# The opening of a Fourier-mixing and ELU kernel: batch 0 folded by mirrored rows first, and its order of work written anew

## The chip, the cores and the metric

The kernel runs on one core of a Trainium2 chip. The metric is device time in microseconds (us) of one execution. The engines are TensorE (PE, matmuls), VectorE (DVE), ScalarE (ACT), GpSimd (POOL) and SyncE (SP, which here issues most of the DMA transfers). Each engine takes its instructions from a queue of its own in the order in which the program wrote them; waits between engines go by semaphores.

## The reference

```python
X = np.fft.fft(x, axis=1)              # x: 8 batches, 3008 rows, 256 channels
X = np.fft.fft(X, axis=2)
y = X.real.reshape(24064, 256)
h = y @ w_in                           # 256 x 2048
g = np.where(h > 0, h, np.exp(np.minimum(h, 0)) - 1)
out = g @ w_out                        # 2048 x 256
```

Two facts are used. The real part of the two-dimensional transform depends only on x[s, d] + x[-s, -d], rows and channels taken modulo 3008 and 256. And it is even under (k, c) -> (-k, -c), so half of the output rows can be had from the other half by a sum and a difference. The weights come as 64-bit floats and are converted in the kernel.

## The kernel before

**Transform along the rows.** A batch is loaded as four tiles L[0] to L[3] (`xl0` to `xl3`), each 128 partitions by six rows of 256 channels: row s ahead from 0, rows back from 3008, rows back from 1504, rows ahead from 1504. L[0] and L[3] are loaded by SP; L[1] and L[2], whose rows run backwards, by GpSimd's indirect DMA (line 239). Each tile comes in two transfers, one of four rows of a partition (512 KB) and one of two ("few", 256 KB). The tiles are *folded* over channels (e: channel d plus channel 256-d, o: the difference) and over the four quarters of the rows, giving four tiles of 128 by 768: cosine and sine, for even and odd output rows. Each is then multiplied with its matrix `MC` (four matrices, 128 by 1887 columns) in two halves of three products: "even" (189, 189 and 378 columns) and "odd" (three of 377 or 376 columns). Channel 128 has a transform of its own, `x`, with one column as the stationary operand. The results are unfolded by VectorE (copy, sum, up, down) into rings `Rr`, `Ir` and `Rb` of eight tiles of 256 columns.

**Transform along the channels** is folded into the weights: every chunk of 256 columns of w_in (eight chunks, w0 to w7) is multiplied with a small matrix `CC` (step f), and the result is copied by ScalarE into `Ws` and `Wc`; its last row goes to `wex`.

**Weights.** A chunk is loaded as pairs of 32-bit words and converted by a chain: top (a) and mantissa (b) on VectorE, power (p), low (l) and high (d) on ScalarE, round (R), sign (s) and multiply (M), pair (P). Round and multiply are on GpSimd for all chunks but w0, whose chain is on VectorE and ScalarE. The chunks of w_out are u0 to u7. `w0a` is the top of chunk w0, `f0` its product with CC, `Wc0` and `Ws0` the copies, `wm0` and `wex0` its last row. Buffers for raw words and powers are shared among chunks, so that a chunk can wait for one before it.

**Steps.** The rest is 376 steps (tile of 256 tokens times slice of 256 hidden columns, eight slices per tile): P (Wc times Rr), V (the even part E on VectorE, `even_part`, line 1263), Q (Ws times Ir, added to P), h (2E minus the sum), b+ and b- (ReLU of the negative, ScalarE), x+ and x- (exponential, ScalarE), g+ and g- (ELU, VectorE), and then Xa and Xb, the products with w_out. For the first two tiles these are plain; from the third on a Winograd form with sums on GpSimd. In the first sixteen steps the two first tiles alternate.

**Order.** Every operation is a function put into a list with a due time in us; the list is sorted by due time and written out, each function pinned in program order. `PERIOD` (4.8) is the length of a step. For the opening, the table `FRONT` gives 40 due times from -20.84 to 33.32 with the names of operations; what stands ahead of it, written directly, are 46 warm-up matmuls on zeros, the loads of batch 0, w0, CC and the first matrix, and w1. The other loads (`load_rest`) stand at -11.63 behind a one-element copy on ScalarE that reads the last of the loaded rows. Later chunks of weights get their steps at offsets -0.5, 0.05, 0.06 and 2.95 from a step's start. Batch 1 is folded on GpSimd (`mirror_folds`), by mirrored rows first; batches 2 to 7 by a finer split of the rows.

The folds of batch 0 in `fold_x` go over channels first, each tile for itself (e0 to e3, o0 to o3, 768 columns each, e0 and e2 cut in two), then over rows (E0, E2, O0, O2 between two tiles, EO0 to EO3 between the pairs), all on VectorE. `mm` is the helper of all matmuls (line 539), `vtt` (545), `gtt` (548) and `act` (551) those of VectorE, GpSimd and ScalarE.

Of the kernel before, what the change touches and what calls it, by code (L numbers as in the profile page):

```python
# [9 lines left out]
FP = mybir.dt.float32  # L10
# [5 lines left out]
ALU = mybir.AluOpType  # L16

SEQ = 3008
ND = 256
# [15 lines left out]
BS = 4  # L35

# [126 lines left out]
def kernel(  # L163
# [64 lines left out]
    def load_x(b):  # L228
# [20 lines left out]
        def ahead(j, row):  # L249
            nc.sync.dma_start(out=L[j][:, 0 : 4 * ND], in_=xrows(b, row, 4, 128, 4))  # L250
            nc.sync.dma_start(
                out=L[j][:, 4 * ND :], in_=xrows(b, row + 512, 2, 128, 2)
            )

        loads = [lambda n=n: back(2 - n // 2, n % 2) for n in range(4)]
        return L, loads + [lambda: ahead(3, HALF), lambda: ahead(0, 0)]
# [238 lines left out]
    def load_mats(ri, kodd, cuts=()):  # L495
        n = (2 * ri + kodd) * BW
        ends = (0, *cuts, BW)
        for a, z in zip(ends, ends[1:]):
            nc.sync.dma_start(
                out=MC[ri, kodd][:, a:z], in_=MC_dr.ap()[:, n + a : n + z]  # L500
            )
# [128 lines left out]
    def fold_x(L, engine_of, cuts_of):  # L630

        ops = {}

        def op(key, o, a, b, f):
            tt = lambda o, a, b, f: pin(
                engine_of(key).tensor_tensor(out=o, in0=a, in1=b, op=f)  # L636
            )
            cuts = cuts_of(key, o.shape[1])
            for i in range(len(cuts) - 1):
                c = slice(cuts[i], cuts[i + 1])  # L640
                ops[key, i] = lambda c=c: tt(o[:, c], a[:, c], b[:, c], f)

        E, O = [], []
        for j in range(4):
            e = spool.tile([128, 6 * 128], FP, tag=f"e{j}", bufs=1, name=f"e{j}")
            o = spool.tile([128, 6 * 128], FP, tag=f"o{j}", bufs=1, name=f"o{j}")
            ev, ov = (
                t.rearrange("p (m o d) -> p m o d", o=2, d=64) for t in (e, o)
            )
            src = L[j].rearrange("p (m d) -> p m d", d=ND)  # L650
            if j in (1, 2):
                src = src[:, ::-1]

            lo, hi = (
                t.rearrange("p m (d o) -> p m o d", o=2)
                for t in (src[:, :, 1:129], src[:, :, 255:127:-1])
            )
            op(f"e{j}", ev, lo[:, :, ::-1], hi[:, :, ::-1], ALU.add)
            ops[f"c{j}", 0] = lambda e=ev[:, :, 0, 63:64], s=src[:, :, 0:1], j=j: (
                act(e, s)  # L660
                if engine_of("c") is nc.vector and j != 1
                else pin(engine_of("c").tensor_copy(out=e, in_=s))
            )
            op(f"o{j}", ov, lo, hi, ALU.subtract)
            E.append(e)
            O.append(o)
        ops["x1", 0] = lambda: act(L[1][0:1, 5 * ND :], L[0][0:1, 0:ND])
        op("E0", E[0], E[0], E[1], ALU.add)
        op("E2", E[2], E[2], E[3], ALU.add)
        op("EO0", E[1], E[0], E[2], ALU.add)  # L670
        op("EO1", E[3], E[0], E[2], ALU.subtract)
        op("O0", O[0], O[0], O[1], ALU.subtract)
        op("O2", O[2], O[2], O[3], ALU.subtract)
        op("EO2", O[1], O[0], O[2], ALU.subtract)
        op("EO3", O[3], O[0], O[2], ALU.add)
        return [E[1], E[3], O[1], O[3]], ops
# [144 lines left out]
    def fold_first(L):  # L821

        c = [t.rearrange("p (m d) -> p m d", d=ND)[:, :, 128:129] for t in L]
        c[1], c[2] = c[1][:, ::-1], c[2][:, ::-1]
        a = spool.tile([128, 6], FP, tag="xa", bufs=1, name="xa")
        g = spool.tile([128, 6], FP, tag="xg", bufs=1, name="xg")
        vtt(a.unsqueeze(2), c[0], c[1], ALU.add)
        vtt(g.unsqueeze(2), c[2], c[3], ALU.add)
        d = state["x_odd"] = spool.tile([128, 6], FP, tag="xd", bufs=1, name="xd")
        vtt(d, a, g, ALU.subtract)  # L830
        e = spool.tile([128, 6], FP, tag="xe0", bufs=1, name="xe0")
        vtt(e, a, g, ALU.add)
        return e


# [9 lines left out]
    def dft_mms(ps, ri, kodd, par, stat, width):  # L845
        for j, (m, c, n, o) in enumerate(dft_parts(ri, kodd, par)):
            mm(
                ps[:, o : o + n],
                stat[:, m * width : m * width + 128]
                if width > 1  # L850
                else stat[:, m : m + 1].to_broadcast([128, 128]),
                MC[ri, kodd][:, c : c + n],
                j == 0,
                j == 2,
            )
# [23 lines left out]
    class Dft:  # L879
# [7 lines left out]
        def mms(self, par, ps):  # L887
            dft_mms(ps, self.ri, self.kodd, par, self.stat, 1 if self.first else 128)
            if par:
                self.odd = ps  # L890
            else:
                self.even = ps
# [667 lines left out]
    for _ in range(46):  # L1560
# [3 lines left out]
    for load in loads[:5]:  # L1564
        load()
    w1_chunks[0].load()
    loads[5]()
    nc.sync.dma_start(out=CC, in_=CC_dr.ap())
    load_mats(0, 0, (BE,))
    w1_chunks[1].load()  # L1570
    nc.sync.dma_start(out=pick, in_=PK_dr.ap())
    EO, ops = fold_x(
        L_first,
        lambda key: nc.vector,
        lambda key, n: (0, 4, n) if key in ("e0", "e2") else (0, n),
    )

    def dft_now(d, par, tag):
        d.mms(par, bank(tag))

    R_even, I_even = Dft(0, 0, 0, EO[0]), Dft(1, 0, 0, EO[2])
    R_odd, I_odd = Dft(0, 0, 1, EO[1]), Dft(1, 0, 1, EO[3])
# [7 lines left out]
    def load_rest():  # L1590

        ops["x1", 0]()
        act(MC[1, 0][0:1, 0:1], L_first[1][0:1, 0:1])
        load_mats(1, 0)
        w2_chunks[0].load()
        w1_chunks[2].load()
        load_mats(0, 1)
        for chunk in (w1_chunks[3], w2_chunks[1], w1_chunks[4], w2_chunks[2]):
            chunk.load()
        load_mats(1, 1)  # L1600
        w1_chunks[5].load()
        w2_chunks[5].load()

    def open_x(b):
        state["L"], state["loads"] = load_x(b)

    def begin_x_even():
        state["x_even"] = Dft(0, 0, 0, fold_first(L_first), ring=Rb, first=True)

    def copy_row(cols):  # L1610
# [9 lines left out]
        ("xs", begin_x_even),  # L1620
        ("xl1", load_rest),
# [4 lines left out]
    for (key, i) in list(ops):  # L1626
        names[key + "ab"[i] if key in ("e0", "e2") else key] = ops[key, i]
    for c in range(6):
        for name, chunk in ((f"w{c}", w1_chunks[c]), (f"u{c}", w2_chunks[c])):
            for key, fn in zip(  # L1630
                "abpldRsMP",
                (chunk.top, chunk.mantissa, chunk.power, chunk.low, chunk.high,
# [7 lines left out]
        names[f"wex{c}"] = lambda c=c: put_last_row(c)  # L1640
    for k, d, tags in (
        ("x", lambda: state["x_even"], ("pC", "pD")),
        ("R", lambda: R_even, ("pA", "pB")),
        ("I", lambda: I_even, ("pC", "M")),
# [368 lines left out]
```

## Time and profile before

| | |
|---|---|
| median of 4 runs | 1916.61 us (1916.3 to 1917.04) |
| the profiled execution | 1916.5 us |
| its span (first to last instruction) | 1914.7 us |
| PE busy | 1905.9 us |
| DVE / POOL / ACT busy | 1431.6 / 1351.2 / 878.5 us |
| granted TensorE clock, mean | 0.999 |
| moved by DMA | 71.88 MB |

In rows of a timeline the columns are start and duration in us, engine, line, operation, output and inputs, shape, count, and in brackets the idle time of the engine before the row and what ended it. Rows of the chain that ended last give start, duration and what the end was waiting for. In a group row, durations in ns stand as minimum, median and maximum. A 32-bit matmul is two passes in the trace, so that a group of three products counts six. The end of a matmul is modelled. The time outside the span, 1.8 us, lies around the instructions.

### The profile page before, as it was taken

How to read it: one execution, taken by the hardware profiler on the slowest of the kernel's cores; microseconds unless marked ns; L12 is line 12 of the kernel's file. 1: busy time of each engine (PE TensorE's matmuls, PEld its weight loads, DVE VectorE, ACT ScalarE, POOL GpSimd, SP SyncE). 2: the span in 40 equal slices, each digit the busy share in tenths (PEclk: the TensorE clock that was granted, in tenths of full speed). 3: DMA queues.
4: the chain of work that ended last, by engine and by line, in shares of the span. 5: the costliest groups of instructions: out<-in, count | busy, mean ns of one | idle time of the engine just before them, and what ended most of it. 6: DMA issues, size and time to landing. Idle time of an engine off the chain costs nothing.

```text
span 1914.7 us, 27564 instructions
## 1 busy us (share of the span) xinstructions
PE 1905.9 (100%) x8972; PEld 1656.9 (87%) x8972; DVE 1431.6 (75%) x2714; ACT 878.5 (46%) x1712; POOL 1351.2 (71%) x1837
## 2 busy tenths in 40 slices
PE   9999999999999999999999999999999999999999
PEld 6888888888888888888888888888888888888887
DVE  8766667877777777777777777777777777767666
ACT  5754444444444444444444444444444444344443
POOL 4888667776687766777667776687766776556665
PEclk9999999999999999999999999999999999999999
DMA  8146212111021110211102111022110210100101
GB/s 338 45 33 44 55 30 61 32 29 27 12 52 30 31 28 12 51 33 28 26 19 45 36 27 25 12 52 44 24 20 12 54 21 15 17 12 15 20 12 23
DMA packets 271072, 71.88 MB, mean 38 GB/s; under 512 B 256814, under 2 KB 257730, under 8 KB 270928
## 3 DMA queue, kind: packets, MB, share of 16 engines
q1 hardware_dynamic: 257296, 57.34, 15.2%
q0 software_dynamic: 11456, 12.52, 2.2%
q8 instruction: 71, 1.16, 0.3%
q14 instruction: 73, 0.60, 0.1%
q10 hardware_dynamic: 2176, 0.26, 0.1%
HBM read 45.20 MB, written 24.80 MB: 37 GB/s over the span
## 4 chain that ended last, share of the span: by engine, by line
PE 97%; DVE 2%; DMA 0%; issue 0%; ACT 0%; POOL 0%; POOLq 0%; DVEq 0%
PE H L539 38%; PE pB L539 17%; PE pD L539 17%; PE pC L539 17%; PE pA L539 9%; DMA xl<-in_x_dram,ix 0%; DVE e L636 0%; DVE o L636 0%; POOL w L548 0%; DVE E L1263 0%; DVE pow L407 0%; DVE w L365 0%; DVE v L545 0%; DVE ot L1451 0%; DVE u L545 0%
## 5 line engine op out<-in xcount | busy, mean ns | idle before, releaser
L548 POOL TENSOR_TENSOR G<-G 128x256 f32<-128x256 f32 x1440 | 1048.1, 737 | 509.6 <-DVE G L1293 350.3
L551 ACT ACTIVATE G<-H 128x512 f32<-128x512 f32 x376 | 224.8, 598 | 929.7 <-DVE G L1277 926.0
L1263 DVE SCALAR_TENSOR_TENSOR E<-Rb,wex,H 128x256 f32<-128x256 f32 x752 | 328.0, 477 | 373.3 <-PE H L539 366.9
L539 PE MATMUL H<-Rr,Wsc 128*128 128x256 f32 x1504 | 387.3, 380 | 0.6 <-ACT Wsc L551 0.6
L539 PE MATMUL H<-Ir,Wsc 128*128 128x256 f32 x1504 | 386.7, 380 | 1.0 <-DVE E L1263 1.0
L539 PE MATMUL pC<-G,WT 128*128 128x256 f32 x1440 | 369.5, 379 | 0.0
L539 PEld LDWEIGHTS H<-Ir,Wsc 128*128 128x128 f32 x1504 | 278.8, 189 | 48.4 <-DVE E L1263 3.1
L539 PEld LDWEIGHTS H<-Rr,Wsc 128*128 128x128 f32 x1504 | 282.6, 190 | 41.7 <-issue 2.3
L539 PEld LDWEIGHTS pC<-G,WT 128*128 128x128 f32 x1440 | 273.6, 190 | 37.2
L1277 DVE SCALAR_TENSOR_TENSOR G<-E,H 128x512 f32<-128x512 f32 x376 | 257.3, 684 | 46.6 <-POOL G L548 13.1
L1293 DVE SCALAR_TENSOR_TENSOR G<-G,H 128x512 f32<-128x512 f32 x376 | 256.3, 682 | 40.8 <-ACT G L551 40.6
L1293 DVE SCALAR_TENSOR_TENSOR G<-M,G 128x512 f32<-128x512 f32 x376 | 257.4, 685 | 0.7 <-ACT M L551 0.7
L551 ACT ACTIVATE G<-G 128x512 f32<-128x512 f32 x376 | 233.4, 621 | 0.0
L539 PE MATMUL pB<-G,w 128*128 128x256 f32 x784 | 229.3, 379 | 0.0
L539 PE MATMUL pA<-G,w 128*128 128x256 f32 x784 | 229.3, 379 | 0.0
L539 PE MATMUL pD<-G,w 128*128 128x256 f32 x784 | 229.2, 379 | 0.0
L551 ACT ACTIVATE M<-G 128x512 f32<-128x512 f32 x376 | 224.1, 596 | 2.8 <-DVE G L1277 2.8
L551 ACT ACTIVATE M<-M 128x512 f32<-128x512 f32 x376 | 221.1, 588 | 0.1
L539 PE MATMUL pB<-G,WT 128*128 128x256 f32 x720 | 214.4, 379 | 0.0
L539 PE MATMUL pD<-G,WT 128*128 128x256 f32 x720 | 214.1, 379 | 0.0
L539 PEld LDWEIGHTS pA<-G,w 128*128 128x128 f32 x784 | 148.9, 190 | 20.5
L539 PEld LDWEIGHTS pB<-G,w 128*128 128x128 f32 x784 | 148.9, 190 | 20.4 <-PE H L539 0.2
(170 smaller groups left out, 1530.9 us busy)
## 6 DMA issues: line engine op xcount, KB each, us to landing
out_dram<-ot SPq DMA_DIRECT2D x496, 32.0 KB
xq<-in_x_dram SPq DMA_DIRECT2D x12, 384.0 KB
out_dram<-ot SPq DMA_DIRECT2D x256, 2.0 KB
xq<-in_x_dram SPq DMA_DIRECT2D x12, 320.0 KB
Rb<-r SPq DMA_DIRECT2D x10, 376.0 KB
raw<-in_moe_w_in_dram SPq DMA_DIRECT2D x7, 512.0 KB
MC<-dft_mats SPq DMA_DIRECT2D x3, 943.5 KB
xl<-in_x_dram SPq DMA_DIRECT2D x4, 512.0 KB
```

Source lines behind the costliest of these rows:

```text
L539: nc.tensor.matmul(out_, lhsT=lhsT, rhs=rhs, start=start, stop=stop, skip_group_check=True)
L548: pin(nc.gpsimd.tensor_tensor(out=o, in0=a, in1=b, op=op))
L551: pin(nc.scalar.activation(out=o, in_=i, func=func, **kw))
L1263: nc.vector.scalar_tensor_tensor(out=S.E[:, c], in0=Rb[:, cols(i)], scalar=wex[:, f : f + 1], in1=S.H[:, c], op0=ALU.mult, op1=ALU.add,)
L1277: nc.vector.scalar_tensor_tensor(out=two(S.G[:, 0:512])[:, :, ::-1], in0=two(S.E), scalar=2.0, in1=two(S.H), op0=ALU.mult, op1=ALU.subtract,)
L1293: nc.vector.scalar_tensor_tensor(out=o, in0=e, scalar=-1.0, in1=h, op0=ALU.add, op1=ALU.max)
```

## The change

Batch 0 is now folded by mirrored rows first: row s of L[3] gets channel -d of its mirror in L[2] added, L[0] that of L[1], in place ("y2", "y0"); then L[0] plus L[3] ("Z", even output rows) and L[0] minus L[3] ("Zd", "Ze", odd output rows); then the channel folds e and o of both. Mirror sums, sums and folds for the even rows are cut by rows of a partition: "a" rows 1 and 3, "b" rows 0 and 2, "c" rows 4 and 5. The first transforms are cut the same way: "x-odd1" and "R-odd1" are the first two of the three products, "x-odd2" the third. The last fold of the odd rows ("om") is on GpSimd. Channel 128 is read straight from the sums; its own four small operations are gone.

The table of due times is replaced by one list of names, written out ahead of all else; the transfers are in it too. The first matrix comes in four pieces, the loads of batch 0 in another order, warm-up matmuls are 30. The I transform's even half takes a bank H in place of pC. Later chunks have their steps at 0.95, 0.96, 0.97 and 2.95.

```diff
+WARM = 30
-        loads = [lambda n=n: back(2 - n // 2, n % 2) for n in range(4)]
-        return L, loads + [lambda: ahead(3, HALF), lambda: ahead(0, 0)]
+        return L, {
+            (j, few): lambda j=j, few=few: (back if j in (1, 2) else ahead)(j, few)
...
-    def load_mats(ri, kodd, cuts=()):
+    def load_mats(ri, kodd, a=0, z=BW):
...
-    def fold_x(L, engine_of, cuts_of):
...
+    def first_folds(L):
+        rows = [t.rearrange("p (m d) -> p m d", d=ND) for t in L]
+        plus, minus = rows[1][:, ::-1], rows[2]
...
+        def mirror(j, m):
+            own, other = rows[j], rows[(1, 2)[j == 3]][:, ::-1]
+            vtt(own[:, m, 1:], own[:, m, 1:], other[:, m, :0:-1], ALU.add)
+            vtt(own[:, m, 0:1], own[:, m, 0:1], other[:, m, 0:1], ALU.add)
+
+        def fold(kodd, ri, m, tt):
+            src = minus if kodd else plus
+            lo, hi = (
+                t.rearrange("p m (d o) -> p m o d", o=2)
+                for t in (src[:, m, 1:129], src[:, m, 255:127:-1])
+            )
+            o = eo[kodd][ri].rearrange("p (m o d) -> p m o d", o=2, d=64)[:, m]
+            if ri:
+                tt(o, lo, hi, ALU.subtract)
+            else:
+                tt(o, lo[:, :, ::-1], hi[:, :, ::-1], ALU.add)
...
+        def add(m):
+            vtt(plus[:, m], rows[0][:, m], rows[3][:, m], ALU.add)
+
+        def even(m):
+            fold(0, 0, m, vtt)
+            edge(0, m, vcopy)
...
+        ops["y2a"] = lambda: mirror(3, near)
+        ops["y2c"] = lambda: mirror(3, rest)
+        for key, m in (("a", odd), ("b", even_), ("c", rest)):
+            ops["y0" + key] = lambda m=m: mirror(0, m)
+            ops["Z" + key] = lambda m=m: add(m)
+            ops["e" + key] = lambda m=m: even(m)
+        ops["oab"] = lambda: fold(0, 1, near, vtt)
+        ops["oc"] = lambda: fold(0, 1, rest, vtt)
+        for key, c in (("Zd", slice(0, 3 * ND)), ("Ze", slice(3 * ND, 6 * ND))):
+            ops[key] = lambda c=c: vtt(L[2][:, c], L[0][:, c], L[3][:, c], ALU.subtract)
+        ops["em"] = lambda: fold(1, 0, every, vtt)
+        ops["cm"] = lambda: edge(1, every, act)
+        ops["om"] = lambda: fold(1, 1, every, gtt)
+        ops["x1"] = lambda: act(L[1][0:1, 5 * ND :], L[0][0:1, 0:ND])
...
-    def dft_mms(ps, ri, kodd, par, stat, width):
+    def dft_mms(ps, ri, kodd, par, stat, width, some=range(3)):
...
-    for _ in range(46):
+    for _ in range(WARM):
...
-    for load in loads[:5]:
-        load()
-    w1_chunks[0].load()
-    loads[5]()
-    nc.sync.dma_start(out=CC, in_=CC_dr.ap())
-    load_mats(0, 0, (BE,))
-    w1_chunks[1].load()
-    nc.sync.dma_start(out=pick, in_=PK_dr.ap())
+    for few in range(2):
+        for j in (2, 1):
+            loads[j, few]()
...
-        ("I", lambda: I_even, ("pC", "M")),
+        ("I", I_even, ("H", "M")),
...
-    FRONT = (
-        (-20.84, "e3 o3"),
...
-    )
+    FRONT = """
+        x3a x0a x3b y2a m0a x0b w0g m0b cc m0d x1 y0a pk Za y0b m0c ea w1g m1 w2g
+        x-odd1 Zb m2 R-odd1 y2c oab y0c eb x-even1 Zc w0a u0g R-even1 w0p ec x-even2
+        Zd x-odd2 R-even2 w4g u5g w0b w0s R-copy m3 R-odd2 w0R oc w0M Ze f0 I-even
+        x-copy R-sum w1b Ws0 u2g Wc0 w1d R-up x-sum em w1a w1l P0 I-copy w2b R-down
+        I-sum x-up wm0 w2l wex0 cm w1R w3g x-down Irc V0 w5g I-odd w1p u1g I-up
+        O-even R4 xd w1s u0a u0b Q0 w2d h0 Irc2 u0l om P1 w1M O-copy O-odd V1 u0p
+        u0d b+0 u3g x+0 I-down w1P L b-0 f1 u0s w2a Ws1 Wc1 u0R g+0 Q1 w2R wm1 x-0
...
+    """.split()
+    for n, name in enumerate(FRONT):
+        at(n - 1000, names[name])
...
-        for dt, fns in zip((-0.5, 0.05, 0.06, 2.95), chunk.steps()):
+        for dt, fns in zip((0.95, 0.96, 0.97, 2.95), chunk.steps()):
```

In the list, x3a to x0b are loads of L[3] and L[0] (a: four rows, b: two), m0a to m0d the pieces of the first matrix (two odd blocks, the first two even blocks, the third even block, the third odd block), m1 to m3 the other matrices, cc and pk small tables, and a name ending in g the load of a chunk.

## The prediction

> **What bounds the kernel now.** I read the page first, then the timeline of TensorE for the first 130 us, then the chain of waits over the same stretch, then VectorE's timeline.
>
> ```profile
> PE 1905.9 (100%) x8972; PEld 1656.9 (87%) x8972; DVE 1431.6 (75%) x2714; ACT 878.5 (46%) x1712; POOL 1351.2 (71%) x1837
> ...
> PE 97%; DVE 2%; DMA 0%; issue 0%; ACT 0%; POOL 0%; POOLq 0%; DVEq 0%
> ```
>
> TensorE is the bound, and the chain that ended last is its own for 97%. The change adds and removes no real matmul, so it can only move time in which TensorE does no real work. That time is in the opening:
>
> ```profile
> 1.14 11.74 PE L539 MATMUL M<-zero 128*128 128x512 bf16 x46 [1.14 <-DVE zero L526]
> 13.26 1.97 PE L539 MATMUL H<-w,CC 128*128 128x256 f32 x8 [0.39 <-DMA CC<-chan_mats]
> 15.91 1.55 PE L539 MATMUL pC<-MC,xe 128*128 128x189 f32 x6 [0.69 <-DVE xe L545]
> ...
> 19.92 2.17 PE L539 MATMUL pB<-MC,e 128*128 128x377 f32 x6 [0.22 <-DVE e L636]
> ...
> 34.80 0.61 PE L539 MATMUL H<-pick,Wsc 128*128 128x1 f32 x4 [0.61 <-ACT Wsc L551]
> ...
> 59.79 1.13 PE L539 MATMUL H<-Rr,Wsc 128*128 128x256 f32 x4 [0.55 <-ACT Wsc L551]
> ...
> 101.19 1.13 PE L539 MATMUL H<-Ir,Wsc 128*128 128x256 f32 x4 [0.72 <-DVE E L1263]
> ```
>
> The first row is warm-up on zeros; real work begins at 13.26. After it there are five stalls over 0.2 us. A row's end holds about 0.14 us of drain that the next matmul overlaps (eight passes last 1.89 us, the next row starts 1.73 later), so a stall costs its idle time plus 0.14: the first four cost 2.07 + 0.56 = 2.6 us, the one at 101 us 0.86. This caps the change: with the same start and no stall at all the time would be 1916.5 - 3.5 = 1913.0.
>
> What sets the start is in the chain and on VectorE:
>
> ```profile
> 3.17 7.73 DMA xl<-in_x_dram,ix
> 10.92 0.43 DVE e L636
> 11.35 0.87 DVE o L636
> ```
>
> ```profile
> 5.19 0.96 DVE L636 TENSOR_TENSOR e<-xl 128x768 f32<-128x768 f32 x1 [4.11 <-DMA xl<-in_x_dram]
> 6.07 0.95 DVE L636 TENSOR_TENSOR o<-xl 128x768 f32<-128x768 f32 x1
> ...
> 12.13 0.69 DVE L636 TENSOR_TENSOR e<-xl 128x512 f32<-128x512 f32 x1
> ...
> 99.05 0.43 DVE L353 TENSOR_SCALAR pow<-raw 128x512 int32<-128x512 int32 x1 [2.17 <-POOL w L548]
> 99.39 0.96 DVE L365 TENSOR_SCALAR w<-raw 128x512 int32<-128x512 int32 x1
> 100.27 0.86 DVE L1263 SCALAR_TENSOR_TENSOR E<-Rb,wex,H 128x256 f32<-128x256 f32 x2
> ```
>
> The mirrored rows come by GpSimd's indirect loads, issued at 1.74, 3.17, 4.43 and 5.68 us and landing 8.1, 7.7, 8.3 and 8.1 later: 9.8, 10.9, 12.7 and 13.8. From 10.9 on VectorE runs without a break. Before that it has already done 4.9 us of work that needs no mirrored row (two folds, the first weight chunk, part of a third fold).
>
> **The change, part by part.** VectorE's durations follow from the rows' spacing: 768 columns 0.87 us, 512 columns 0.60, 256 columns 0.34, six columns 0.08; an operation that needs the one just before it starts 0.12 later (xg at 15.42, xd at 15.62).
>
> Folds. Removed: 16 operations of 768 columns, 13.9 us. Added on VectorE: mirror sums 3.9, quarter sums 3.5, channel folds 0.9 + 1.6 + 0.9, together 10.9; one fold of 768 goes to GpSimd. That saves 3 us, but the new order needs a mirrored row in its very first operation, so VectorE idles to 9.8 and the 4.9 us done early are done late. I lay the rows end to end. The indirect loads now go large, large, small, small; between 9.84 and 12.7 they brought 0.79 MB, 0.27 MB per us, so the second large one lands at 11.8 and the small ones at 12.7 and 13.8. y2a 9.9 to 11.1; y0a waits to 11.8, ends 12.5; Za ends 13.2: x-odd1 starts at 13.3, as late as real work starts now. Then y0b 13.9, ea 14.4, Zb 15.0, y2c 15.7, oab 16.3, y0c 17.0, eb 17.5, Zc 18.1, w0a 18.5, ec 19.0, Zd 19.9, w0b 20.2, w0s 20.8, w0R 21.4, oc 21.7, w0M 22.3.
>
> TensorE. Three products of 377 columns take 1.90 us (23.21 to 25.11), an even half 1.28. x-odd1 13.3, R-odd1 14.6, x-even1 15.9 to 16.5; R-even1 needs eb, so it waits to 17.6: **a new stall of 1.1**. x-even2, x-odd2, R-even2, R-odd2 end at 20.8. f0 needs w0M, which stands behind all these folds on VectorE: it starts at 22.5, **a new stall of 1.7**. f0 to 24.2, I-even to 25.5. P0 needs Wc0, two copies of 0.53 on ScalarE after f0: 0.1. Then wm0, I-odd, O-even, Q0, P1, O-odd, f1, Q1 go on without a wait to 35.4; wm1 waits for the copies of f1, as now: 0.5. On to 60 us nothing else waits by the rows. New stalls 3.4 against 2.6: **+0.8**.
>
> Steps of the later chunks. Their first operation moves from 0.5 ahead of a step to just behind its even part. The stall at 101 us is exactly that: pow of one chunk waits 2.17 for GpSimd's multiply of the chunk before (same buffer), and the even part E, which TensorE needs, stands behind it in VectorE's queue. In the new order E stands ahead: **-0.86**. What waits instead are the ELU operations behind it, which have over 2 us before their matmuls. The chunks' GpSimd work comes 1.45 us later, ahead of f7, with about 2 us in hand. Bounds: nothing saved, or all 0.86.
>
> Loads. SP's transfers are rewritten as one list, x first, then matrices in the order of use. With all queues about 0.40 MB per us flow from 2 us on (392 to 415 GB/s in the windows from 10 to 40 us). Counting the bytes ahead, the second cosine pieces (4.6 MB) land at about 14.4 against a need at 18.9, the sine matrix (6.3 MB) at 18.7 against 24.2, the third (7.8 MB) at 22.4 against 28.7. Cost nothing, covered by at least 4 us. SP issues run further ahead than now and wait only for landings eight transfers earlier, where bytes are still queued behind them.
>
> GpSimd. One fold of 768 columns at 2.6 ns (128x384 in 1.0 us): 1.9 us, between round and multiply of chunk 1, whose f1 is due at 33.7. By the rows (round 1.3, fold 1.9, multiply 1.3, two pairs 1.4, from 26 us) it is ready at 33: 0.7 in hand. Bounds 0 to 1.3, the length of one such operation if ScalarE hands over late; I take 0.
>
> Warm-up. 16 zero matmuls fewer end it at 12.9 - 16 x 0.217 = 9.4. The end is on no path. But TensorE then idles 3.9 us, which this trace never shows. The rows of the warm-up:
>
> ```profile
> L539 PE MATMUL M<-zero x4: 634/634/634, 1.5 to 2.8; 128*128 128x512 bf16 x4
> L539 PE MATMUL M<-zero x6: 378/379/379, 5.7 to 6.8; 128*128 128x512 bf16 x6
> ```
>
> The first nine or so, to 4.3 us, are spaced 0.43 and the rest 0.217: the first 3.2 us run at half speed, though the granted clock reads 1.00. If idling brings that back, 3.2 us of matmuls from 13.3 on take double, and 1.6 of the delay falls into the stalls before R-even1 and f0: 0 to 0.8. If the slow state holds until TensorE is busy without a break, the 6.4 us of transforms ahead of f0 take 12.8 and f0 starts at 26.1 in place of 22.5: 3.6, and up to 1.7 more while f0 itself is slow; I price that case between, at 4.6. I take 0; the stalls in today's opening, up to 0.69 us, leave no slow row behind.
>
> [...]
>
> Sum against the profiled execution (1916.5 us, span 1914.7): +0.04 start, +0.8, -0.86: **1916.5**. The median of the runs, 1916.61, is 0.1 above it.
>
> **Rivals.** Faster: the two new stalls are shorter, since VectorE's real spacing or the first indirect landing is better than laid out; with both halved and the stall at 101 gone, 1916.5 - 1.4 = 1915.1, without them 1913.7. For it: the load order feeds VectorE earlier than 10.9. Against: the landings are set by GpSimd's four issues, which stay where they are.
>
> Later waits: the new list puts conversions where they hold TensorE up, at f1 (1.3 as bounded), and the stall at 101 stays (0.86): 1918.7. For it: 0.5 to 0.7 us in hand at f1. Against: the same work, and the rows fit.
>
> Slow clock, the other side: 1916.5 + 4.6 = 1921.1, decided by whether the 3.9 us of idling reset the clock and the stalls at 16.5 and 20.8 keep it from being released; it would be seen as x-odd1 taking 2.6 us instead of 1.3. Against: 0.69 us stalls now do nothing.
>
> **How the numbers follow.** Forecast 0.54 (1915.6 to 1917.4); faster rival 0.18; later waits 0.19; slow clock 0.09. The range 1914.3 to 1919.4 leaves out the far end of the faster case (0.06) and the slow clock (0.09) with a little of the later waits. A measurement of this kernel can tell about 0.2% from no change, 3.8 us: 1912.8 and 1920.4. The cap of 1913.0 leaves 0.03 for faster; slower 0.09, the slow clock; same 0.88.
>
> **What would show it.** First real matmul at 13.3; waits of about 1.1 before R-even1 and 1.7 before f0, both on VectorE; no wait at 101 us; matmuls of 377 columns at 478 ns from the start. Wrong if TensorE's waits in the first 60 us sum to under 2 or over 4.5 us, or if those rows last about 1 us.

## The result

The changed kernel is slower: median 1919.62 us of 32 runs (1918.95 to 1921.59) against 1916.78 of 52 runs of the kernel before, ratio 1.0016 with a 95% interval of 1.0011 to 1.0021. The forecast was 1916.5 with a range to 1919.4. The 32 runs lie in two groups, 17 up to 1919.63 and 15 from 1920.54 on, with medians 1.7 us apart (1919.34 and 1921.07); a fall of TensorE's clock, described below, costs 1.58 in the profile and is taken to set them apart. The profiled execution, 1920.69 us with a span of 1918.8, belongs to the upper group. One run of those below is left out of its kernel's figures: the sixth of e9, 2502.26 us at a granted clock of 0.752.

### The profile page after: what moved, and what is told of

The parts are those of the page before. It is cut to its first block, busy times and chain, and to the rows that moved or that the text cites. A ratio compares the mean times of both kernels' runs of the same rounds, so it can differ in the third digit from the quotient of the medians.

```text
span 1918.8 us, 27532 instructions
## 1 busy us (share of the span) xinstructions
PE 1905.6 (99%) x8956; PEld 1657.2 (86%) x8956; DVE 1430.4 (75%) x2715; ACT 877.6 (46%) x1710; POOL 1350.6 (70%) x1838
## 3 DMA queue, kind: packets, MB, share of 16 engines
q8 instruction: 71, 1.16, 0.3%
## 4 chain that ended last, share of the span: by engine, by line
PE 96%; DVE 2%; DMA 1%; POOL 1%; issue 0%; ACT 0%; SPq 0%; DVEq 0%; POOLq 0%
PE H L544 38%; PE pB L544 17%; PE pC L544 17%; PE pD L544 17%; PE pA L544 9%; DMA xl<-in_x_dram,ix 0%; DVE xl L550 0%; POOL w L553 0%; DVE pow L362 0%; DVE E L1280 0%; DMA wx<-Wsc 0%; DVE w L374 0%; DMA wex<-wx 0%; DVE v L550 0%; DVE e L550 0%
```

## The profile after

The page's busy times and its chain of waits, for the rows shown of before:

```profile
PE 1905.6 (99%) x8956; PEld 1657.2 (86%) x8956; DVE 1430.4 (75%) x2715; ACT 877.6 (46%) x1710; POOL 1350.6 (70%) x1838
...
PE 96%; DVE 2%; DMA 1%; POOL 1%; issue 0%; ACT 0%; SPq 0%; DVEq 0%; POOLq 0%
```

The real matmuls are the same: 8956 instructions, and the 16 warm-up matmuls left out make the 8972 of before. Those 16 took some 3.5 us (16 x 0.217), yet the busy time falls by 0.3 only. So the 4.1 us of span are time in which TensorE did nothing, or did its work slowly. TensorE's timeline shows where:

```profile
12.73 1.53 PE L544 MATMUL pD<-MC,xl 128*128 128x377 f32 x4 [3.54 <-DVE xl L550]
14.10 2.64 PE L544 MATMUL pB<-MC,e 128*128 128x377 f32 x4
...
17.70 0.81 PE L544 MATMUL pA<-MC,e 128*128 128x189 f32 x4
...
21.82 1.99 PE L544 MATMUL H<-w,CC 128*128 128x256 f32 x8 [0.78 <-DVE w L430]
...
35.73 0.60 PE L544 MATMUL H<-pick,Wsc 128*128 128x1 f32 x4 [0.42 <-ACT Wsc L556]
37.24 2.95 PE L544 MATMUL H<-Rr,Wsc 128*128 128x256 f32 x8 [0.91 <-DVE G L1310]
...
103.45 1.03 PE L544 MATMUL H<-Ir,Wsc 128*128 128x256 f32 x4
...
116.45 1.13 PE L544 MATMUL H<-Ir,Wsc 128*128 128x256 f32 x4 [1.61 <-DVE E L1280]
```

I hold the same matmul of both kernels side by side; the last column is how far the changed kernel is behind.

| operation | before | after | behind |
|---|---|---|---|
| first real matmul | 13.26 | 12.73 | -0.53 |
| wm1, last row of chunk w1 | 34.80 | 35.73 | 0.93 |
| f2 (0.87 of four matmuls moved ahead of it taken off) | 40.54 | 45.05 | 3.64 |
| first product with Wc ahead of J-even | 59.79 | 63.00 | 3.21 |
| Q that stalled before | 101.19 | 103.45 | 2.26 |
| Q that stalls now | 112.64 | 116.45 | 3.81 |
| last block of small matmuls | 1908.01 | 1911.88 | 3.87 |

So the opening up to wm1 costs 0.93, the next ten us 2.7, then 0.4 comes back where before waited at 59.79, 0.95 where it waited at 101.19, and the new wait at 116.45 costs 1.6. From there on the two kernels run alike to the last block; behind the last matmul the changed kernel takes another 0.2 to the end of its span.

The 2.7 are two things. P3 waits 0.91 (1.05 with the drain) for g+0, which frees its PSUM bank (a buffer that matmuls write into); and the eight passes of P3 and P2 take 2.74 and the eight of the product behind them 2.47, where eight take 1.73 elsewhere. The windows of the profile show why: a row gives the stretch and its length, then busy time of PE, PEld, DVE, ACT and POOL, the granted clock, and the DMA's share and GB/s.

```profile
9.00:13.00 4.00, 0.46 (x2) 0.27 (x2) 3.08 (x6) 0.41 (x1) 0.00 (x0) 1.00 1.03 407
...
14.00:15.00 1.00, 1.00 (x3) 0.70 (x3) 1.00 (x3) 0.00 (x0) 0.00 (x0) 0.59 1.09 377
15.00:16.00 1.00, 1.00 (x3) 0.42 (x2) 1.00 (x4) 0.00 (x0) 0.00 (x0) 0.50 1.13 442
...
39.00:40.00 1.00, 1.00 (x4) 0.73 (x4) 0.41 (x1) 1.00 (x3) 0.44 (x1) 0.50 0.77 274
40.00:41.00 1.00, 1.00 (x4) 0.82 (x3) 0.77 (x2) 1.00 (x3) 0.92 (x2) 0.50 0.09 35
41.00:42.00 1.00, 1.00 (x5) 0.86 (x4) 1.00 (x4) 0.55 (x2) 1.00 (x2) 0.76 0.02 4
```

The clock fell to one half twice, each time for about 3.4 us: after TensorE had idled from 9.19 to 12.73, and again behind the two waits at 35.73 and 37.24. In the kernel before it reads 1.00 in every window up to 140 us. From P3 to f2 the changed kernel needs 7.81 us; in a run without the second fall (e3 below) the same matmuls take 6.72, of which 0.49 is a wait. The second fall costs 1.58, close to the 1.7 between the two groups of runs.

Why is g+0 late? VectorE's timeline, first two conversions of the opening and then the stretch ahead of g+0:

```profile
19.21 0.42 DVE L374 TENSOR_SCALAR w<-raw 128x512 int32<-128x512 int32 x1
19.54 0.68 DVE L416 SCALAR_TENSOR_TENSOR pow<-raw,pow 128x512 int32<-128x512 int32 x1
...
29.21 1.01 DVE L416 SCALAR_TENSOR_TENSOR pow<-raw,pow 128x512 int32<-128x512 int32 x1
...
30.49 1.50 DVE L374 TENSOR_SCALAR w<-w 128x512 int32<-128x512 int32 x1
...
33.75 1.32 DVE L416 SCALAR_TENSOR_TENSOR pow<-w,pow 128x512 int32<-128x512 int32 x1
34.99 1.51 DVE L362 TENSOR_SCALAR pow<-raw 128x512 int32<-128x512 int32 x1
36.42 0.68 DVE L1310 SCALAR_TENSOR_TENSOR G<-G,H 128x512 f32<-128x512 f32 x1
```

and GpSimd's in the same stretch:

```profile
27.50 2.18 POOL L553 TENSOR_TENSOR o<-xl 128x768 f32<-128x768 f32 x1
30.37 1.33 POOL L553 TENSOR_TENSOR w<-w,pow 128x512 f32<-128x512 f32 x1 [0.70 <-DVE pow L416]
...
33.22 1.29 POOL L553 TENSOR_TENSOR w<-w 128x512 f32<-128x512 f32 x1
34.48 1.74 POOL L553 TENSOR_TENSOR w<-raw,w 128x512 f32<-128x512 f32 x1
```

VectorE never idles from 27 to 38 us. The same integer conversions take 0.42 (lines 362 and 374) and 0.68 (line 416) where GpSimd is idle, as at 19.21 and 19.54. Each long one ends 0.3 to 0.6 us after the GpSimd operation that was running when it was issued: 30.49 + 1.50 = 31.99 after 30.37 + 1.33 = 31.70. Together the four are 3.1 us longer than alone.

The wait at 116.45, in the chain of waits:

```profile
107.28 0.08 POOL rx L553
...
109.23 1.15 DMA r<-rx
...
110.40 0.34 SPq L1231
...
110.79 0.28 SPq L1235
...
111.12 2.18 DMA wx<-Wsc
...
113.37 2.05 DMA wex<-wx
```

SP issues in the order r, Rb, Ir, wx, wex. GpSimd's rx comes late, so wx, whose source ScalarE has written by 110.63, is issued only at 111.12, and right behind the broadcast Rb it takes 2.18 us. In the kernel before rx was done by 104.0 and wx, issued alone, took 1.1:

```profile
108.44 0.23 SPq L588 DMA_DIRECT2D wx<-Wsc  x1
109.56 0.38 SPq L591 DMA_DIRECT2D wex<-wx  x1
```

## The experiments

The kernel before ran beside them on the same chip: 1916.42 with e1, e2, e3 and b1, 1916.54 with e4, e5, e6 and b2, 1916.52 with e7, e8, e9 and b3, 1916.56 with o1, o2, o3 and b4, 1916.65 with o4 and b5. Times are medians of eleven runs if nothing else is said. Names with b are edits of the kernel before, all others of the changed kernel.

### The warm-up: e1 and b1

```diff
-WARM = 30
+WARM = 46
```

> The changed kernel with 46 warm-up matmuls again instead of 30, nothing else altered. In the profile of the changed kernel TensorE idles from 9.19 to 12.73 us and the granted clock then falls to 0.5 from 14 to about 17.4 us; a second such fall, from 38 to 41.5 us, follows the stalls of 0.42 and 0.91 at 35.7 and 37.2. Theory A (hidden): with 46 the first fall is gone, but R-even1 waits for VectorE's quarter fold anyway and starts at 17.7 as before, so the time stays within 0.4 us of the changed kernel and the second fall stays. Theory B (the warm-up is the loss): the time drops by 1.5 to 3 us and the rest of the opening moves forward with it. Theory C: both falls share one cause, and the second goes with the first: minus 1.7.

1919.44 (1918.88 to 1920.86). The first fall is gone (the clock reads 1.00 in every window up to 140 us), and the time is the same:

```profile
1.14 12.45 PE L544 MATMUL M<-zero 128*128 128x512 bf16 x46 [1.14 <-DVE zero L531]
17.25 0.91 PE L544 MATMUL pA<-MC,e 128*128 128x189 f32 x4 [0.48 <-DVE e L673]
22.05 1.99 PE L544 MATMUL H<-w,CC 128*128 128x256 f32 x8 [1.36 <-DVE w L430]
```

What the clock gives back is lost at once: the longer warm-up starts the real work at 13.43 in place of 12.73, and the waits ahead of R-even1 and f0 end when VectorE is ready. Theory A holds in the main: the first fall was hidden (R-even1 moved to 17.25, not 17.7). In this profile the second fall is absent, too, though P3 waits the same 0.91. But two of the eleven runs lie 0.8 us and more above the rest, with a granted clock of 0.999 where the other nine have 1.000; one fall of 3.4 us takes 0.0009 off that mean. o1 below settles theory C: its profile has a second fall and no first.

```diff
-    for _ in range(46):
+    for _ in range(30):
```

> The kernel before with 30 warm-up matmuls instead of 46, nothing else altered. Its warm-up then ends at about 9.2 us and its first real matmul needs the matrices at 13.26, so TensorE idles about 4 us. Theory A (idling of 3.5 us or more lets the clock fall for about 3.4 us from the next window on): the granted clock reads 0.5 for 3 us or so between 13 and 18 us, and as VectorE's folds follow close behind in that kernel the time rises by 0.5 to 1.7 us. Theory B (the fall in the changed kernel has another cause, the pattern of its small products): the clock stays at 1.00 and the time within 0.3 of before.

1917.67 (1916.39 to 1918.56), 1.25 above before, with an interval of the ratio that reaches 1 (0.9995 to 1.0013); by rows wm1 is 1.16 late (35.96). The clock reads 0.50 from 13 to over 18 us, and the first weight fold, 1.97 us before, takes 3.75:

```profile
12.91 3.75 PE L539 MATMUL H<-w,CC 128*128 128x256 f32 x8 [3.03 <-DMA CC<-chan_mats]
```

The four runs with a mean clock of 0.999 (as one length of 3.4 us gives it) have a median of 1916.81, the seven with 0.998 (two lengths, as in the profile) 1917.72: the longer the fall, the dearer. So the same cut costs up to 1.3 where VectorE follows close behind TensorE, and next to nothing where TensorE waits for VectorE anyway. TensorE had idled 3.03 us, where theory A has 3.5 or more; the "next window" of that theory is shown by no run.

### P3's wait: e3 and e4

```diff
-b-0 f1 u0s w2a Ws1 Wc1 u0R g+0 Q1
+b-0 f1 Ws1 Wc1 u0R g+0 u0s w2a Q1
```

> The changed kernel with the list's names u0s and w2a (two integer conversions on VectorE) moved from ahead of g+0 to just behind it. In the changed kernel they last 1.32 and 1.51 us, ending 0.3 to 0.5 after a GpSimd operation that began before them, and hold g+0 to 36.42; P3 on TensorE needs the PSUM bank that g+0 frees. Theory A (conversions held by GpSimd, then head of the queue): g+0 ends 1 to 1.5 us earlier, P3's wait of 0.91 goes, TensorE no longer idles 1.3 us in the stretch from 35 to 38, the clock stays at 1.00 from 38 to 42, and the time falls by 2 to 2.8 us. Theory B (g+0 waits for ScalarE's exp, not for VectorE): P3 starts at 37.2 all the same and the time stays within 0.4. Theory C (the bank wait goes but the clock's fall is bound to the time since the start or the first fall): P3's wait goes, the clock still falls near 38, minus 0.9.

1919.04, and all eleven runs lie between 1918.73 and 1919.48. g+0 begins at 34.04 in place of 36.42, P3 goes without a wait, and TensorE next waits 0.35 for g-0:

```profile
36.33 1.97 PE L544 MATMUL H<-Rr,Wsc 128*128 128x256 f32 x8
38.66 1.97 PE L544 MATMUL pA<-G,w 128*128 128x256 f32 x8 [0.35 <-DVE G L1310]
```

The second fall is in no run's time. Without it the gain is small. Held against e1, which has no second fall either, TensorE is 0.55 ahead at f2 (1.05 of P3's wait against 0.49 for g-0) and 0.50 at 112 us; then the wait at 115 grows from 1.41 to 1.76 and leaves 0.16. VectorE's queue stays the limit at P3; only what stands at its head changes. The runs also price the first fall: five with a clock of 1.000 have a median of 1918.81, five with 0.998 one of 1919.17, so 0.4 for twice 3.4 us.

```diff
-u0l om P1
+u0l P1
...
-Xb0 g+1 h2
+Xb0 g+1 om h2
```

> The changed kernel with om, the one fold that GpSimd does, moved in the list from ahead of P1 to behind g+1, some 12 us later. In the changed kernel om holds GpSimd from 27.50 to 29.68 and the conversion of line 416 at 29.21 lasts 1.01 us instead of 0.68. Theory A (om is what makes g+0 late, so that P3 waits for its PSUM bank): conversions between 29 and 35 are shorter by 0.8 us or more together, P3's wait of 0.91 falls under 0.3, the second fall of the clock goes, the time falls by 0.7 to 2.5. Theory B (the round and multiply operations of the chunks hold the conversions whatever om does): only the operation at 29.21 is shorter, P3's wait stays at 0.5 to 0.9 and the time within 0.4.

1919.53 (1919.17 to 1919.87). Theory B: the operation at 29.28 lasts 0.69 in place of 1.01, the other three long ones stay long, P3 waits 0.69.

```profile
29.28 0.69 DVE L416 SCALAR_TENSOR_TENSOR pow<-raw,pow 128x512 int32<-128x512 int32 x1
...
30.22 1.50 DVE L374 TENSOR_SCALAR w<-w 128x512 int32<-128x512 int32 x1
```

That settles what lengthened this conversion: GpSimd's operation taken away, the length goes. For the other three it is argued from where they end. om costs 0.2 to 0.3 here, and where it went it makes f3 wait 0.40 at 56.22. By their times none of these eleven runs, with waits of 0.42 and 0.69, has the second fall; with 0.42 and 0.91 it is 15 of 32 in the changed kernel, two of eleven in e1 and six of eleven in o1.

### The first weight chunk: o1 and e8

o1 has 42 warm-up matmuls, too, and is to be held against e1:

```diff
-x3a x0a x3b y2a m0a x0b w0g m0b
+w0g x3a x0a x3b w0a w0p w0b w0s w0R w0M y2a m0a x0b m0b
```

(w0a, w0p, w0b, w0s, w0R and w0M are taken out of their later places.)

> The changed kernel with 42 warm-up matmuls, and with the first weight chunk loaded ahead of the x rows and converted on VectorE ahead of the first fold; TensorE's order as it is. To be held against e1_warm46 (same, with the chunk converted between the folds: f0 waits 1.36, P3 0.91). Theory A (VectorE's queue from 9.2 us on makes the opening): VectorE reaches its first anti sum 1 to 2.5 us earlier, f0's wait of 1.36 goes or falls under 0.3 and the time falls by 1.0 to 2.5 us against e1's 1919.4. Theory B (R-copy on ScalarE and the x rows 1.3 us later take its place): f0 still starts within 0.5 of 22.05 and the time stays within 0.5 of 1919.4.

1918.98, in two groups: five runs from 1917.67 to 1918.19 at a clock of 1.000, six from 1918.98 on at 0.999, with P3 slow in the profile again (3.47). Between the lower groups it is 1.57 faster than e1 (1917.75 against 1919.32). f0 waits for nothing:

```profile
20.55 1.89 PE L544 MATMUL H<-w,CC 128*128 128x256 f32 x8
...
34.34 0.60 PE L544 MATMUL H<-pick,Wsc 128*128 128x1 f32 x4 [0.42 <-ACT Wsc L556]
35.85 3.47 PE L544 MATMUL H<-Rr,Wsc 128*128 128x256 f32 x8 [0.91 <-DVE G L1310]
```

wm1 comes 1.62 ahead of e1 and 0.46 ahead of the kernel before. Theory A: the opening's loss is VectorE's conversion of that chunk between the folds, after it stood idle until 9.2. P3's wait of 0.91 moves along unchanged, so it is not the end of the queue of folds; it is made between 27 and 36 us.

e8 does the same with 30 warm-up matmuls and puts f0 behind x-even1:

> The changed kernel with one weight chunk, the first, loaded ahead of the x rows on SP and converted on VectorE ahead of the first fold, and f0 put behind x-even1 on TensorE. In the changed kernel VectorE does nothing until 9.17 us, then folds without a break, and its five operations on that chunk (2.6 us) stand between the folds, so that f0 starts at 21.82. Theory A (the opening is bound by VectorE's queue from 9.2 on, and P3's wait is the end of that queue): f0 fills the wait ahead of R-even1, I-even starts 1.2 to 2.8 us earlier than 23.65, P3's wait falls under 0.4, and the time falls by 1.5 to 3.5 us, to 1916 to 1918. Theory B (x lands later by the chunk's 0.5 MB, about 1.3 us at 0.4 MB per us, or the slow clock now falls on real work that nothing hides): the start moves to 13.5 to 14 and the time falls by less than 1.

1924.28 (five runs, 1922.58 to 1927.16), a miss. The slow clock (0.50 from 14 to 18 us) now lies on work that nothing hides, and f0 (1.73) delays R-even2, so that VectorE waits 3.57 for ScalarE's copy; then two conversions that take 0.42 alone take 1.53 and 2.38:

```profile
24.20 0.62 DVE L550 TENSOR_TENSOR bs<-pA,anti 128x189 f32<-128x189 f32 x2 [3.57 <-ACT anti L556]
...
26.91 1.53 DVE L362 TENSOR_SCALAR pow<-raw 128x512 int32<-128x512 int32 x1
28.36 2.38 DVE L374 TENSOR_SCALAR w<-raw 128x512 int32<-128x512 int32 x1
```

That GpSimd holds these two is my estimate from the changed kernel's rows, since no row of GpSimd in e8 shows it. TensorE then waits 3.45 at 33.92, and its clock falls a second time (0.50 from 34 to 38 us).

### The offsets of the later chunks: e2, b2, e5, b5

```diff
-zip((0.95, 0.96, 0.97, 2.95), chunk.steps())
+zip((-0.5, 0.05, 0.06, 2.95), chunk.steps())
```

> The changed kernel with the four offsets of the later chunks' steps put back to -0.5, 0.05, 0.06, 2.95 (they are 0.95, 0.96, 0.97, 2.95). Theory A (the move only exchanged one wait for a dearer one): the stall of 1.61 us at 116.45, where E waits for the transfer of wex, is gone or under 0.3, the stall of 0.7 at 101 us is back at its place (about 104 now), and the time falls by 0.6 to 1.2 us against the changed kernel. Theory B (the wait at 116 comes from the opening running 3 us late, not from the offsets): the stall at 116 stays at 1.3 to 1.6 and the one at 101 comes on top: plus 0.7 to 0.9.

1919.37 (1918.75 to 1920.84): no gain. The wait at 116 goes and the one at 101 comes back, at 105.05 with 0.88 (1.02 with the drain), and 0.25 more before it. By rows the new offsets lose 0.2 in this kernel.

In the kernel before, the other way round (0.95, 0.96, 0.97):

> The kernel before with the new offsets of the later chunks' steps (0.95, 0.96, 0.97, 2.95 instead of -0.5, 0.05, 0.06, 2.95), nothing else altered. Theory A (the move only exchanges one wait for another): the stall of 0.72 at 101 goes, rx on GpSimd comes over 2 us later and holds SP's queue, and a new wait of 0.8 to 1.7 for wex appears at 112 to 113; the time goes up by 0 to 0.9. Theory B (the prediction's reading: the operations have room): no new wait, minus 0.86.

1916.62 (1916.09 to 1916.87) against 1916.54: nothing, where the prediction had -0.86. The wait at 101 is gone and another stands for it:

```profile
112.87 1.13 PE L539 MATMUL H<-Ir,Wsc 128*128 128x256 f32 x4 [1.26 <-DVE E L1263]
```

with r at 105.70, wx at 107.59 taking 2.18, as in the changed kernel, although ScalarE has written its source by 107.09. The exchange of waits is the edit's own and does not need the late opening.

e5 issues r, Rb and Ir of batch 0 on SP behind wx and wex, pinned there:

```diff
-    at(11 * T + 3.6, lambda: spread_ext(0, 1))
+    at(13 * T + 0.1, lambda: (put_rows(1, 1), spread_ext(0, 1)))
```

(put_rows is the transfer r, taken out of ext_rows.)

> The changed kernel with one change on SP's queue: the last weight row's two transfers wx and wex are issued ahead of the three that spread the extra channel's row (r, Rb, Ir), which wait for GpSimd's rx, instead of behind them. In the changed kernel r is issued at 109.23, wx only at 111.12 though its source was written at 110.63, and wx takes 2.18 us where it takes 1.12 in the kernel before. Theory A (SP's order makes the wait at 116): wx is issued at about 110.7, wex lands 1.3 to 1.5 us earlier, the stall of 1.61 falls to 0.1 to 0.4, the time falls by 1.2 to 1.6. Theory B (the chain through ScalarE's copy of the last row sets it): wx leaves at 110.7 but the stall stays over 1.1, minus 0.4 at most.

1919.04 (1918.35 to 1922.14), 0.6 less between the lower groups (1918.73 against 1919.34). The wait at 116 is 0.35, wx takes 1.10; the span's end comes 7.7 us after the start of the last block of small matmuls, 6.9 in the changed kernel, which takes back 0.8. Theory A for the wait, with a price at the end whose cause no run shows.

b5 has the same edit and the new offsets in the kernel before:

> The kernel before with the new offsets of the later chunks' steps and with wx and wex ahead of r, Rb and Ir on SP. Theory A (SP's order makes the wait that the new offsets bring): the wait of 1.26 at 112.87 of b2 falls under 0.4, and the time is 1915.5 to 1916.1 in most runs, with some runs 3 us higher if the extra channel's loads come late again as in e6, or 0.7 higher all along if the last stores wait as in e5 and e6 (their spans ended 7.7 us after the last block of small matmuls began, in the others 6.9). Theory B (the chain through ScalarE sets it): the wait stays over 0.8, 1916.3 to 1916.8.

**1915.46** (1914.76 to 1917.10) against 1916.65: 1.2 less, ratio 0.9992 with an interval of 0.9983 to 1.0001. Eight of its eleven runs lie under the lowest of the 21 runs of before. It is the fastest version of this study, though the interval just reaches 1. SP's queue in it:

```profile
107.22 0.24 SPq L588 DMA_DIRECT2D wx<-Wsc  x1
108.33 0.36 SPq L591 DMA_DIRECT2D wex<-wx  x1
108.78 0.28 SPq L1193 DMA_DIRECT2D r<-rx  x1
```

The wait at 111.80 is 0.51 in place of b2's 1.26, so SP's order made 0.75 of that. By rows this is less than the 1.2 of the medians. The profile is 0.38 ahead of the kernel before at 15.53 already, ahead of anything that the edit touches, and gains 1.01 more where the wait at 101 was; 0.55 comes back at 111.80. That leaves 0.46 for the edits there, a little over half of the 0.86 that the prediction gave the offsets. The rest of the 1.2 is not accounted for. SP's order without the new offsets was not run in the kernel before; its trace leaves that order 0.12 to gain at 112.64, where Q starts 1.85 after a product that takes 1.73.

### The extra channel's row elsewhere: b3, e7, o3, b4

b3 (the kernel before with the new offsets) and e7 (like e6 below) issue r, Rb and Ir of batch 0 from GpSimd's queue:

```diff
-            nc.sync.dma_start(
+            (nc.sync if b else nc.gpsimd).dma_start(
```

> The kernel before with the new offsets of the later chunks' steps, as in b2_new_offsets, and with r, Rb and Ir of the first batch on GpSimd's queue, so that SP issues wx as soon as its source is written. In b2 the stall of 0.72 at 101 was gone and one of 1.26 at 112.87 stood in its place. Theory A (that wait is SP's order and nothing else): it falls under 0.4 and the time is 0.6 to 1.3 below b2's 1916.6, the first gain over the kernel before. Theory B (GpSimd's issues delay its own chunk work by as much): within 0.4 of 1916.6.

> As e6_three_mended (42 warm-up matmuls, g+0 ahead of two conversions), but r, Rb and Ir of the first batch are issued from GpSimd's queue in place of SP's, so that they are not deferred and SP has nothing ahead of wx. In e6 the wait at 116 was gone but the later loads of the extra channel came 3 us later on SP and one run showed a new wait of 3.12 at 195. If that was the price of deferring, the time is 1917.6 to 1918.3 with no wait at 116 or 195; if GpSimd's issues cost as much as they free, it is 1918.5 to 1919.5.

1919.15 and 1919.99: worse. GpSimd is held 3.3 us by the three issues, 1.36 of it waiting for r to land, its chunk is late, and a product with w_out waits 1.88 and 2.13 for it. In b3 the clock falls behind that wait as well (a mean of 0.91 from 100 to 120 us; in e7's profile it is 1.00):

```profile
111.83 2.87 PE L539 MATMUL pA<-G,w 128*128 128x256 f32 x8 [1.88 <-POOL w L548]
```

b4 (the kernel before, new offsets) and o3 (42 warm-up matmuls, g+0 first) leave the transfers on SP and compute the row on VectorE:

```diff
-    at(11 * T + 3.54, lambda: ext_unfold(1, gtt, 1))
-    at(11 * T + 3.55, lambda: ext_rows(1, gtt, 1))
+    at(11 * T + 0.93, lambda: ext_unfold(1, vtt, 1))
+    at(11 * T + 0.94, lambda: ext_rows(1, vtt, 1))
```

> The kernel before with the new offsets of the later chunks' steps and the four operations that make the extra channel's row on VectorE instead of GpSimd. Theory A: no wait at 101 and none over 0.3 at 112 to 113, so 0.6 to 1.1 below the kernel before, 1915.4 to 1916.0. Theory B (the 1.8 us more on VectorE make a wait of their own): 1916.3 to 1917.5.

> The changed kernel with 42 warm-up matmuls, g+0 ahead of two conversions, and the four operations that make the extra channel's row on VectorE instead of GpSimd. Theory A (GpSimd's backlog holds rx, rx holds SP, SP holds wx): r, Rb and Ir leave SP about 100 to 104 us, wx as soon as its source is written, the wait of 1.4 to 1.8 at 115 falls under 0.3, and the time is 1917.2 to 1918.0. Theory B (wex is bound by ScalarE's copy and the two transfers): the wait stays at 0.8 or more, 1918.5 to 1919.

1917.87 and 1920.01: also worse. r leaves SP at 96.84 in b4, wx goes alone and takes 1.10, yet the wait is 1.23 (1.61 in o3). The chain now goes through VectorE and ScalarE:

```profile
104.31 1.70 DVE pow L407
106.02 0.61 DVE G L1277
...
108.77 0.50 ACT Wsc L551
109.28 0.60 ACT Wsc L551
...
109.90 1.10 DMA wx<-Wsc
```

VectorE's conversion of line 407 takes 1.70 there (0.69 alone), and ScalarE's copy of the last row ends at 109.87, in the kernel before at 108.42. That GpSimd, relieved, takes up the next chunk just then is my estimate; no row of b4 shows it. So theory B holds here: the edit itself lengthened the chain through ScalarE. What that chain costs undisturbed is b5's 0.51.

### Sums: e6, e9, o2, o4

e6 is 42 warm-up matmuls, e3 and e5 together:

> The changed kernel with three edits together: 42 warm-up matmuls, g+0 ahead of the two conversions, and wx and wex ahead of r, Rb and Ir on SP. If the three losses are what they seem and add up (0.3 for g+0 in runs without the second fall, 1.2 to 1.6 for the wait at 116, nothing for the warm-up), the time is 1917.2 to 1918.0, still 0.8 to 1.5 above the kernel before, and all runs lie in one group because no fall of the clock is left. If the warm-up's fall costs more than it seems, or the losses hide one another, it is under 1916.5 or over 1918.5.

1918.65 (1917.90 to 1926.14; nine of the eleven up to 1919.48). P3's wait and the one at 116 are gone, none is left between 60 and 130 us. But the profiled run, 1921.6 and the second highest, shows a new one, for the extra channel's transform of batch 1:

```profile
194.98 2.32 PE L544 MATMUL H<-MC,xe 128*8 128x189 f32 x24 [3.12 <-POOL xe L553]
```

In the chain ahead of it a load of x takes 10.85 us to land. That SP's new order delays it is a guess: the profiles of e5, b5 and o4, with the same order, show no wait there.

e9 is e8, e3 and GpSimd's queue; o2 is o1, e3 and the row on VectorE; o4 is o1, e3 and e5:

> The changed kernel with the first weight chunk converted ahead of the folds, g+0 ahead of the two conversions, and r, Rb and Ir of the first batch on GpSimd's queue. If the losses add up (1.5 to 3.5 for the opening, 1.2 to 1.6 at 116), the time is 1914.5 to 1916.5, level with the kernel before or 2 us under it. If they hide one another, 1917 to 1918.5.

> As o1_w0_early, with g+0 ahead of two conversions and the four operations that make the extra channel's row of the first batch on VectorE, behind an even part, in place of GpSimd. If the three add up: 1.0 to 2.5 from the chunk, 0.3 from g+0, 1.2 to 1.9 at 116, so 1915.0 to 1917.0. If VectorE is too full between 30 and 40 us or near 100, new waits there leave it at 1917.5 or more.

> The changed kernel with 42 warm-up matmuls, the first weight chunk converted ahead of the folds, g+0 ahead of two conversions, and wx and wex ahead of r, Rb and Ir on SP. If the waits taken away add up (from o1's 1917.8 in its runs without a fall of the clock: 0.3 for g+0, 1.3 to 1.8 at 115, less 0.7 for the last stores): 1916.2 to 1916.9, level with the kernel before. If VectorE and GpSimd collide elsewhere as in o2: 1917.5 or more.

1923.47 (five runs, 1922.13 to 1927.04), 1918.72 and 1922.28. e9 inherits e8's wait of 3.45 and GpSimd's of 2.09. o2 inherits the wait at 114 (1.20). o4 splits: five runs from 1916.64 to 1917.67 with a median of 1916.88, level with the kernel before and about where its terms add up, and six from 1922.28 to 1923.53; the profile shows a run of the lower group (span 1915.7). What the upper group waits for isn't in a trace; the loads of the extra channel, as in e6, are a guess.

## Why the prediction was wrong

**The warm-up's term.** The prediction took 0 and reasoned that stalls of up to 0.69 leave no slow row behind. The clock fell all the same. The sign that it had named for its slow-clock rival came one group later than named (R-odd1, two products of 377 columns, 2.64 us where e1 has 1.43). The cost stayed within the prediction's own bounds for a short fall, 0 to 0.8, and for the reason given there: the delay falls into the waits for VectorE (nothing in e1, 0.4 in e3). The rival's 4.6, for a slow state that lasts, did not come; the falls end after 3.4 or 6.8 us. So the 0 was near the truth by luck, since it stood for no fall at all. The second fall, 1.58 us in the profile and by the times in 15 of the 32 runs, was not in the sum.

**"On to 60 us nothing else waits by the rows."** This step failed. It priced P3's wait at nothing; with the drain it is 1.05, and the second fall comes behind it. The prediction writes VectorE's rows out to w0M at 22.3 only. The list puts two conversions ahead of g+0, and I took all conversions at 0.42 and 0.69, their usual lengths between 20 and 70 us in the kernel before; four of them last 3.1 us longer here. e4 shows for one of them that the length is GpSimd's doing (0.69 without om beside it, 1.01 with it), e3 that the order in VectorE's queue makes the wait. The +0.8 of the sum was a balance to 60 us; at 63.00 the kernel is 3.21 behind.

**"Steps of the later chunks: -0.86."** This step failed, too. The wait at 101 did go. In the changed kernel that gave 0.95, and the new wait at 116.45 took 1.55. I asked only which VectorE operations wait in its place, and gave GpSimd 2 us in hand ahead of f7; I did not follow the 1.45 us through GpSimd's rx to SP, where wx and wex stand behind r. b2 measured the edit alone as +0.08. With SP's order set right (b5) the rows keep 0.46 of the gain, because the chain through ScalarE still leaves a wait of 0.51.

**What held.** The opening up to wm1: 35.73 where the rows laid out end at 35.9, with R-even1 at 17.70 (17.6) and f0 at 21.82 (22.5); against the kernel before that is 0.93 late. o1 shows the cause as the prediction laid it out, w0M behind the folds on VectorE. f1 waits for nothing. The fold on GpSimd took 2.18 us where the prediction had 1.9 (its own 2.6 ns a column give 2.0).

What was measured adds up to 0.93 + 1.05 + 1.58 - 0.4 - 0.95 + 1.6 = 3.8, the lag at 116.45; 0.3 more up to the span's 4.1, 0.2 of it behind the last matmul, is not explained. Without the second fall the span's difference is 2.5, against 2.6 between the lower group's median and before (1919.34 - 1916.78).

Of the rivals "later waits" (1918.7) had the kind right, a conversion that holds TensorE up, and both places wrong: f1 had room, and the wait at 101 went.

## What to carry to other kernels

A step that is moved must be followed on every queue that its results pass, to the last DMA behind them: here a wait of 0.86 taken away on VectorE came back as one of 1.26 or 1.61, most of it because SP's queue had a late transfer ahead of the one that mattered. Durations from a trace are durations beside what ran there; where a conversion on VectorE will meet other GpSimd work, take both lengths (here 0.42 and 1.51 for line 362) into the range. Two short waits close together can cost more than their sum through the clock (0.42 and 0.91 brought 1.58 more in the profile here), so price a cluster of them, not each, and expect groups of runs rather than one time.

## What the runs showed of the hardware

The granted clock's falls to one half lasted about 3.4 us (both in the changed kernel) or about 6.8 (the first in e3, e5 and b1, the first two in e8), by the windows' means. In the changed kernel's profile one came behind 1.33 us of idling (0.42 and 0.91 within 2 us); e1's profile has the same two waits and no fall. Behind 0.42 and 0.69, by the times, it came in none of e4's eleven runs. Single waits were no surer: 1.88 in b3's profile brought a fall, 2.13 in e7's and 1.36 ahead of f0 in e1's did not. Nor was the idling behind the warm-up: 2.37 us in e4's profile were followed by a fall, 3.68 in e9's were not. So the length of the idling alone did not decide here, and what did is not shown.

An integer conversion of 128 by 512 on VectorE took 0.42 or 0.69 us alone and up to 2.30 beside GpSimd (in the kernel before, from 102.25, beside GpSimd's rx from 102.10 to 104.00); the four long ones of the changed kernel ended 0.3 to 0.6 after the GpSimd operation. Not every operation on VectorE grew: an even part and an ELU with one operand in PSUM kept 0.43 (each half, at 32.51) and 0.68 (at 36.42) while GpSimd worked. What sets the two kinds apart is not shown.

The transfer wx (1 KB) took 2.18 us right behind the broadcast Rb (376 KB) in the changed kernel and 1.10 alone in e5; three transfers issued from GpSimd's queue took 3.3 us of GpSimd's time in b3, 1.36 of it a wait between the first and the second.
